# V products of two blocks first, the last MLP tile's high and low parts in one half, and twelve dummy products at the end

## The chip, the cores and the metric

One Trainium2 chip, one of its cores. The core has TensorE (PE; its weight loads are shown as PEld), VectorE (DVE), ScalarE (ACT), GpSimd (POOL) and SyncE (SP), which here only issues DMAs. The metric is the device time of one execution in microseconds (us), median of three runs.

## The reference

For x of 2048 tokens by 512, everything in float32:

```python
xn = _layernorm(x)                      # mean and variance over 512, eps 1e-5
q, k, v = split(xn @ wqkv)              # 32 heads of 16
s = softmax(q @ k.T / 4) @ v @ wo
g = silu(gelu(xn @ w1 + b1) @ w2 + b2)  # 1376 hidden columns, tanh gelu
out = x + s * g
```

## The kernel before, in words

**Precision.** A float32 operand is kept as a high part (rounded by ScalarE to the matmul's format) and a low part (operand minus high, by VectorE or GpSimd). A product is three matmuls into one PSUM bank: high x high, high x low, low x high (`mm3`, line 92).

**Start (lines 389 to 553).** x comes in 16 tiles of 128 tokens, four to a block. For each block of tiles VectorE takes the statistics (lines 414, 415), a root and a few short operations (419 to 424, the root by ScalarE at 420), and the normalised tile (428). TensorE transposes it into PSUM (437, `turn`), ScalarE writes the high part (86), VectorE the low part (87). Then come q and k for the first two groups of heads, per block of 512 tokens (455, `q_first`: 24 products), and V for tokens 0 to 511, per tile (`v_tile`, 12 products through line 92). `evac` (368 to 381) copies q/k out of PSUM on ScalarE, takes the low part on GpSimd, and SyncE stores both to scratch in DRAM. Before the first transposes, and behind them, TensorE runs products on an identity matrix (487, `keep_warm`). wv is split by ScalarE (511) and GpSimd (502). `pool_after` (499) is a tiny GpSimd operation that keeps GpSimd waiting for a given normalised tile. The order of the four blocks is: turns of block 0, q/k 0; turns 1, V tile, q/k 1; turns 2, V tile, q/k 2; turns 3; then, behind the loads described next, V tile, q/k 3, V tile.

**SyncE's order.** Every DMA of SyncE is issued in the order of the program. After the stores of q/k block 2 come `load_qs(0)` (line 146, six loads of q rows back from scratch, high and low stacked in 48 rows) and `load_k(0)` for the first 512 keys (line 121, six loads), then the first MLP weights, the next 1024 keys, the stores of q/k block 3, and the last 512 keys.

**Projection stage (lines 556 to 752).** The rest of V, the MLP and the other q/k groups run as pairs of products on the two halves of TensorE's rows, half 0 on rows 0 to 63 and half 1 on rows 64 to 127 (`run`, `mm`, line 583). Between them, one for each five of these products, `fill` puts a score product q x k (line 193, 48 rows of one half, two PSUM banks in turn), whose maximum VectorE takes (199): 590 of the 2048 in this stage, shared between the halves as evenly as possible. TensorE executes in order, so a score product that waits for its q or k rows holds up all behind it. The first score product is the fifth product of the stage. The MLP's hidden columns are 11 tiles of 128; 1376 is 10 x 128 + 96, so the last is padded with 32 zeros. `half` computes a pair of hidden tiles, `evac` applies gelu and splits, and `down` multiplies with w2: two parts for each block and hidden tile, each with two token tiles of three products on either half.

**Attention and end.** Scores again with the maximum folded in (716), exponentials (719, 721), products with V (787), then the output projection (916, 92), the gate (922), the sum with x (927) and the store (928). The last product goes through line 92 into the bank `two`; behind it are two VectorE operations of 256 columns and the store.

Where a row half must wait for the other's write to the same bank, `mm` puts a hold ahead of the product:

```python
        if not first and writer[key][0] != a and writer[key][1] > prog["seen"]:
            hold = nc.tensor.nop().ins
```

Of the kernel before, what the change touches and what calls it, by code (L numbers as in the profile page):

```python
# [16 lines left out]
P = 128  # L17
# [8 lines left out]
F = 1376  # L26
FT = (F + P - 1) // P
GH = 4
NG = H // GH
# [25 lines left out]
def fused(ctx: ExitStack, tc: tile.TileContext, x, wqk, wv, wo, w1, b1, w2, b2, out):  # L55
# [227 lines left out]
    wk = sa.enter_context(tc.tile_pool(name="work_a", bufs=2))  # L283
    b1_sb = xp.tile([P, FT], F32, name="b1_sb")
    b2_sb = xp.tile([P, D], F32, name="b2_sb")
# [47 lines left out]
    W1, W2 = {}, {}  # L333

    def w1_load(j):
        if j < len(pairs):
            for u in pairs[j]:
                kind, n, f = u
                if kind == "m":
                    W1[u] = w_new(w1[f], 2, "raw1")  # L340
                elif f % 2 == 0:
                    W1[n] = w_new(wqk[:, n], 2, "raw1")
# [8 lines left out]
    def w2_load(i):  # L351
        if i < len(ms):
            W2[ms[i][1:]] = w_new(w2[ms[i][2]], 2, "raw2")

# [9 lines left out]
    def evac(us, ph):  # L364
        raws = [wk.tile([P, CH], F32, name="hg", bufs=2) for u in us]
        for u, raw in zip(us, raws):
            if u[0] == "m":
                nc.scalar.activation(raw, ph.pop(u), AF.Gelu_apprx_tanh, bias=b1_sb[:, u[2]:u[2] + 1])  # L368
            else:
                nc.scalar.activation(raw, ph.pop(u), AF.Copy)  # L370
        for u, raw in zip(us, raws):
            hh = wk.tile([P, CH], F32R, name="hh", bufs=HB)
            hl = wk.tile([P, CH], F32R, name="hl", bufs=HB)
            nc.scalar.activation(hh, raw, AF.Copy)  # L374
            nc.gpsimd.tensor_sub(hl, raw, hh.bitcast(F32))  # L375
            if u[0] == "m":
                HS[u[1:]] = (hh, hl)
            else:
                rs, cs = slice(u[1] * P, (u[1] + 1) * P), slice(u[2] * CH, (u[2] + 1) * CH)
                nc.sync.dma_start(qk_h[rs, cs], hh.bitcast(F32))  # L380
                nc.sync.dma_start(qk_l[rs, cs], hl.bitcast(F32))
# [7 lines left out]
    with ExitStack() as s1:  # L389
# [20 lines left out]
        ve = wp.tile([P, 5, NT], F32, name="ve")  # L410

        def moments(t):
            st = w1k.tile([P, 6], F32, name="st")
            nc.vector.bn_stats(st, xs[t])  # L414
            nc.vector.bn_aggr(mv[:, t, :], st)

        def rstd(t0, t1):
            v = ve[:, :, t0:t1]
            nc.vector.tensor_scalar(v[:, 0], mv[:, t0:t1, 1], EPS, None, op0=OP.add)
            nc.scalar.activation(v[:, 1], v[:, 0], AF.Sqrt)  # L420
            nc.vector.reciprocal(v[:, 2], v[:, 1])
            nc.vector.scalar_tensor_tensor(v[:, 3], v[:, 2], -0.5, v[:, 2], op0=OP.mult, op1=OP.mult)
            nc.vector.tensor_mul(v[:, 3], v[:, 3], v[:, 0])
            nc.vector.scalar_tensor_tensor(v[:, 4], v[:, 3], 1.5, v[:, 2], op0=OP.add, op1=OP.mult)
# [22 lines left out]

        def q_first(c):
            pq = {}
            for n, (i, j) in enumerate(((0, 0), (0, 1), (1, 0))):  # L450
                for g in range(2):
                    if n == 0:
                        pq["q", g, c] = a_tile((P, CH))
                    for k in range(KT):
                        nc.tensor.matmul(pq["q", g, c], W1[g][i][:, k * P:(k + 1) * P], (xh, xl)[j][c][:, k],  # L455
                                         start=n == 0 and k == 0, stop=n == 2 and k == KT - 1)
            evac(list(pq), pq)

        for t in range(4):
            load_x(t, (nc.sync, nc.scalar)[t % 2])  # L460
        warm = wp.tile([1, 2], F32, name="warm")
        nc.vector.memset(warm, 1.0)
        nc.scalar.activation(warm[:, 1:], warm[:, :1], AF.Sqrt)
# [6 lines left out]
        for t in range(6, XB):  # L470
            load_x(t)
# [16 lines left out]

        keep_warm(25)
        def ln(t, n):  # L490
            for i in range(t, t + n):
                moments(i)
            rstd(t, t + n)
            for i in range(t, t + n):
                norm(i)

        ln(0, NCH)
        def pool_after(t):
            nc.gpsimd.tensor_sub(warm[:, :1], xns[t][:1, :1], xns[t][:1, :1])

        def wv_low(k):
            nc.gpsimd.tensor_sub(wv_l[:, k], wv_r[:, k], wv_h[:, k].bitcast(F32))

        pool_after(NCH - 1)
# [5 lines left out]
        for k in range(KT):  # L510
            nc.scalar.activation(wv_h[:, k], wv_r[:, k], AF.Copy)
        for k in range(KT - 2):
            wv_low(k)
        ln(NCH, NCH)
        consts()
        pool_after(2 * NCH - 1)
        for k in range(KT - 2, KT):
            wv_low(k)
# [31 lines left out]
    load_k(0, c0=CH, n=S - 2 * CH)  # L550
    v_tile(NCH - 2)
    q_first(NCH - 1)
    v_tile(NCH - 1)
    load_k(0, c0=S - CH, n=CH)

    prog.update(n=0, pe=0, seen=0)
    writer = {}
    s_when, row = [], [0]
    def fill(a):
        due = 2 * FILL0 + APART * sum(made)  # L560
        if sum(made) < SOON and row[0] >= due and (made[0] <= made[1]) == (a == 0):
            taken()
            if later and later[0][0] <= 0:
                s_send(later.pop(0)[1])
            whole_units = list(ended)
            s_one(a)
            for u in whole_units:
                s_end0(u)
            tick()

# [17 lines left out]
    def run(ops, hooks={}):  # L588
        for n, two in enumerate(zip(*ops)):
# [4 lines left out]
            for h in hooks.get(n, []):  # L594
                h()

    PH = {}
# [21 lines left out]
    def down(c, f, part):  # L619
# [4 lines left out]
        h, w = HS[c, f], W2[c, f]  # L624
        side = (part + i) % 2
        ops = [[], []]
        for a in range(2):
            for t in ((0, 1), (2, 3))[(a + side) % 2]:
                ts = slice(t * P, (t + 1) * P)
                for n, (x, y) in enumerate(((0, 0), (0, 1), (1, 0))):  # L630
                    ops[a].append(((c, t), PA[c][t], h[x][:, ts], w[y],
                                   f == 0 and part == 0 and n == 0, f == FT - 1 and part == 1 and n == 2))
        run(ops)
        if part == 0:
# [446 lines left out]
```

## Time and profile before

| | us |
|---|---|
| median of three runs | 1547.04 |
| the runs | 1546.8 to 1547.23 |
| span of the profiled execution, first to last instruction | 1544.6 |
| TensorE busy | 1538.4 |
| VectorE busy | 1419.2 |
| ScalarE busy | 1212.4 |
| GpSimd busy | 375.8 |

For the profiled execution the page gives the span; the median is 2.4 us more. Times in rows count from the first instruction. A row of the timeline gives start, length, engine, line, operation, output <- inputs, shapes, the count of instructions merged, and in brackets the idle time before it with what ended it. A row of the stages gives the stretch, its length, the busy time and the instruction count of PE, PEld, DVE, ACT and POOL, then the granted TensorE clock, the DMA engines' share and GB/s. TensorE works in a pipeline, so a product's length in a row (0.39 us for 512 columns) is longer than the distance to the next (0.23).

### The profile page before, as it was taken

The page shows a single profiled execution, that of the slowest core. Times are in us where ns is not written, and L with a number is a line of the kernel's source. Part 1 is how long each engine was busy: PE and PEld are TensorE (multiplying, and loading weights), DVE is VectorE, ACT ScalarE, POOL GpSimd, SP SyncE. Part 2 cuts the span into 40 slices and gives each one's busy share as a digit, 9 for nine tenths or more (in the row PEclk, how much of TensorE's full clock was granted, in tenths as well). Part 3 has the DMA queues.
Part 4 walks back from the last instruction along what each step waited for, and adds up shares of the span by engine and source line. Part 5 has one row for each costly group of instructions (what it writes and reads, how often), then busy time and mean ns, then how long its engine had stood idle before and what let it go on. Part 6 is the DMA issues. An engine that isn't in the chain of part 4 may idle for free.

```text
span 1544.6 us, 31302 instructions
## 1 busy us (share of the span) xinstructions
PE 1538.4 (100%) x12230; PEld 922.5 (60%) x12230; DVE 1419.2 (92%) x2294; ACT 1212.4 (78%) x1881; POOL 375.8 (24%) x386
## 2 busy tenths in 40 slices
PE   9999999999999999999999999999999999999998
PEld 8899999999995444444444444444444444444456
DVE  7799999999998999999999999999999999999945
ACT  4333433333339999999999999999999999999994
POOL 4235575756741011001000100100010000000153
PEclk9999999999999999999999999999999999999999
DMA  6615443455422112112411411411051111110162
GB/s 212 155 58 145 124 143 108 120 161 136 141 90 66 39 45 61 33 37 51 75 28 33 71 33 41 60 44 29 21 84 29 32 32 30 41 32 20 50 217 100
DMA packets 78227, 116.83 MB, mean 76 GB/s; under 512 B 28132, under 2 KB 28388, under 8 KB 76904
## 3 DMA queue, kind: packets, MB, share of 16 engines
q1 hardware_dynamic: 73596, 99.80, 23.1%
q0 software_dynamic: 4000, 14.45, 5.0%
q8 instruction: 96, 1.57, 0.4%
q10 hardware_dynamic: 484, 0.60, 0.1%
q14 instruction: 51, 0.42, 0.1%
HBM read 84.35 MB, written 25.97 MB: 71 GB/s over the span
## 4 chain that ended last, share of the span: by engine, by line
PE 99%; DVE 1%; DMA 0%; issue 0%; ACT 0%; DVEq 0%
PE pv L787 33%; PE ps L193 22%; PE ps L583 13%; PE two L716 8%; PE sp L583 5%; PE ps L716 4%; PE pst L716 4%; PE pst L583 3%; PE pv L583 2%; PE ps L916 2%; PE ps L92 1%; PE ps L455 1%; PE pst L92 0%; DVE st L414 0%; PE two L92 0%; DMA xt<-in_x 0%
## 5 line engine op out<-in xcount | busy, mean ns | idle before, releaser
L199 DVE TENSOR_REDUCE mx<-ps 128x2 f32<-128x512 f32 x2048 | 1318.0, 687 | 68.5 <-PE ps L193 18.3
L787 PE MATMUL pv<-slot,vsb 128*32 128x512 f32 x4096 | 543.4, 604 | 0.0
L721 ACT ACTIVATE slot<-two 128x1024 f32<-128x1024 f32 x511 | 520.5, 1019 | 0.0
L193 PEld LDWEIGHTS ps<-kt,slot 48*128 48x128 f32 x1356 | 212.2, 184 | 290.2 <-DVE mx L199 278.4
L193 PE MATMUL ps<-kt,slot 48*128 48x256 f32 (+1 forms) x1356 | 376.3, 366 | 0.0
L719 ACT ACTIVATE slot<-ps 128x512 f32<-128x512 f32 x515 | 307.5, 598 | 16.7 <-PE ps L716 7.2
L719 ACT ACTIVATE slot<-pst 128x512 f32<-128x512 f32 x511 | 309.9, 606 | 0.0
L583 PE MATMUL ps<-slot,w1h 64*128 64x512 f32 x1088 | 225.4, 392 | 0.0
L193 PE MATMUL ps<-kt,qz 48*128 48x512 f32 x512 | 202.2, 395 | 0.0
L716 PE MATMUL two<-qt,kt 50*128 50x512 f32 x766 | 197.5, 395 | 0.3 <-DVE gt L643 0.3
L716 PE MATMUL ps<-qt,kt 50*128 50x512 f32 x387 | 189.7, 492 | 0.0
L193 PEld LDWEIGHTS ps<-slot,slot 48*128 48x128 f32 x590 | 92.8, 184 | 124.0 <-DVE mx L199 118.2
L193 PE MATMUL ps<-slot,slot 48*128 48x256 f32 (+1 forms) x590 | 165.8, 366 | 0.0
L787 PEld LDWEIGHTS pv<-slot,vsb 128*32 128x32 f32 x4096 | 81.5, 108 | 131.9 <-issue 124.4
L583 PEld LDWEIGHTS ps<-slot,w1h 64*128 64x128 f32 x1088 | 154.1, 185 | 9.8
L583 PE MATMUL ps<-slot,w1l 64*128 64x512 f32 x544 | 157.0, 392 | 0.0
L716 PE MATMUL pst<-qt,kt 50*128 50x512 f32 x383 | 155.7, 406 | 0.0
L375 POOL TENSOR_TENSOR hl<-hg,hh 128x512 fp32r<-128x512 f32 x76 | 96.7, 1295 | 158.2 <-ACT hh L374 109.3
L368 ACT ACTIVATE hg<-ps,b_sb 128x512 f32<-128x512 f32 x44 | 27.9, 684 | 133.0 <-PE ps L583 121.7
L716 PEld LDWEIGHTS two<-qt,kt 50*128 50x128 f32 x766 | 114.5, 186 | 1.1 <-DVE gt L643 0.7
L246 POOL CAST mh<-nt 128x32 fp32r<-128x32 f32 x19 | 4.0, 209 | 375.7 <-DVE nt L244 322.8
L193 PEld LDWEIGHTS ps<-kt,qz 48*128 48x128 f32 x512 | 93.7, 183 | 1.0 <-DVE mx L199 0.7
(197 smaller groups left out, 1974.6 us busy)
## 6 DMA issues: line engine op xcount, KB each, us to landing
raw<-in_w SPq DMA_DIRECT2D x88, 256.0 KB
qk_h<-hh SPq DMA_DIRECT2D x32, 256.0 KB
qk_l<-hl SPq DMA_DIRECT2D x32, 256.0 KB
qt<-qk_h SPq DMA_DIRECT2D x128, 64.0 KB
slot<-qk_h SPq DMA_DIRECT2D x92, 64.0 KB
g_d<-gt POOLq DMA_DIRECT2D x16, 256.0 KB, 3.3
qt<-qk_l SPq DMA_DIRECT2D x64, 64.0 KB
dn<-den_d SPq DMA_DIRECT2D x32, 128.0 KB
```

Of the source, the lines that this page charges most:

```text
L92: nc.tensor.matmul(ps, lhs[a], rhs[b], start=first and n == 0, stop=last and n == 2)
L193: return nc.tensor.matmul(ps[:, c0:c0 + w], QS[u][r, p, qi * P:(qi + 1) * P], kts[u // NCH % KB][p][r, k0:k0 + w], start=True, stop=True).ins
L199: nc.vector.tensor_reduce(MX[u][:, 2 * p:2 * p + 2, qi, ki][:, heads, parts], ps.rearrange("p (n c) -> p n c", c=HC), axis=AX.X, op=OP.max)
L368: nc.scalar.activation(raw, ph.pop(u), AF.Gelu_apprx_tanh, bias=b1_sb[:, u[2]:u[2] + 1])
L375: nc.gpsimd.tensor_sub(hl, raw, hh.bitcast(F32))
L455: nc.tensor.matmul(pq["q", g, c], W1[g][i][:, k * P:(k + 1) * P], (xh, xl)[j][c][:, k], start=n == 0 and k == 0, stop=n == 2 and k == KT - 1)
L583: i = nc.tensor.matmul(ps, lhs[r], rhs[r], start=first, stop=last).ins
L716: nc.tensor.matmul(ps, kts[g % KB][p][r, k * P:(k + 1) * P], QT[u][r, p, :], start=True, stop=True)
L719: nc.scalar.activation(PT[u, k][:, 2 * p + a, :], ps, AF.Exp, scale=SCALE)
L721: nc.scalar.activation(PT[u, k][:, :2], TP["two"], AF.Exp, scale=SCALE)
L787: nc.tensor.matmul(PV[u][32 * j:32 * j + 32, :], vsb[:, k, h:h + 32], PT[u, k][:, j, :], start=(k == 0), stop=(k == NT - 1))
L916: HALF[0] = nc.tensor.matmul(PW[i][0], OTS[i, k][x][r], (wo_h, wo_l)[y][r, k], start=k == 0 and side == 0 and n == 0, stop=k == KT - 1 and ...
```

## The change

It has four parts. (1) At the start the first x tile is loaded in two pieces from two queues, wv's pieces are loaded ahead of wqk, statistics are taken for two tiles and then two, with one VectorE operation less, and the V products of the first two token tiles come before q/k block 0, term by term. The other two V tiles come ahead of q/k blocks 1 and 2, and the transposes of block 3 stand inside q/k block 2. (2) The last MLP tile has its 32 last columns twice in one row half: once as high part, once as low part, in the same operand, so that this half needs two products for each token tile instead of three. Its weights come in two arrangements for even and odd blocks. `run_short` orders these steps. (3) In six of the eight steps score products are put into the free places. (4) Twelve products whose result nobody reads stand behind the last real one: three of each of four kinds (128 columns, 64 columns, a broadcast operand, a strided operand).

```diff
+LAST = F - (FT - 1) * P
...
+    def form(c, f):
+        return FT if f == FT - 1 and c % 2 else f
...
             nc.scalar.activation(hh, raw, AF.Copy)
-            nc.gpsimd.tensor_sub(hl, raw, hh.bitcast(F32))
+            if u[0] == "m" and u[2] == FT - 1:
+                long, low = [(slice(0, 64), slice(LAST, P)), (slice(64, P), slice(P - LAST, 64))][u[1] % 2]
+                nc.gpsimd.tensor_sub(hl[long], raw[long], hh[long].bitcast(F32))
+                nc.gpsimd.tensor_sub(hh[low], raw[low], hh[low].bitcast(F32))
+            else:
+                nc.gpsimd.tensor_sub(hl, raw, hh.bitcast(F32))
...
+        def root(t0, t1):
+            nc.scalar.activation(ve[:, 1, t0:t1], mv[:, t0:t1, 1], AF.Sqrt, bias=eps)
...
-        def q_first(c):
+        def v_term(t, n):
+            i, j = ((0, 0), (1, 0), (0, 1))[n]
+            if n == 0:
+                VP[t] = a_tile((P, D))
+            c, ts = t // NCH, slice(t % NCH * P, t % NCH * P + P)
+            for k in range(KT):
+                nc.tensor.matmul(VP[t], (xh, xl)[i][c][:, k, ts], (wv_h, wv_l)[j][:, k],
+                                 start=n == 0 and k == 0, stop=n == 2 and k == KT - 1)
+            if n == 2:
+                v_out(t, VP.pop(t))
+
+        def q_first(c, mid=()):
...
+                    if n == 2 and g == 1:
+                        for t in mid:
+                            turn(t)
...
-        for t in range(4):
-            load_x(t, (nc.sync, nc.scalar)[t % 2])
+        xs[0] = w1k.tile([P, D], F32, name="xt", bufs=XB)
+        for eng, r in ((nc.sync, slice(0, P // 2)), (nc.scalar, slice(P // 2, P))):
+            eng.dma_start(xs[0][r], x[r, :])
+        load_x(1)
+        load_x(2, nc.scalar)
...
+        for k in range(KT):
+            if k == 2:
+                load_x(3)
+            nc.sync.dma_start(wv_r[:, k], wv[:, k])
         for g in range(2):
             W1[g] = w_new(wqk[:, g], 2, "raw1")
-        for t in range(4, 6):
-            load_x(t)
-        for k in range(KT):
-            nc.sync.dma_start(wv_r[:, k], wv[:, k])
...
-        keep_warm(25)
+        keep_warm(15)
...
-        ln(0, NCH)
...
+        moments(0)
+        moments(1)
+        root(0, 2)
+        stats(2)
+        rstd(0, 2)
+        norm(0)
+        norm(1)
+        aggr(2)
+        moments(3)
+        for k in range(KT - 1):
+            wv_high(k)
+        pool_after(1)
+        turn(0)
+        wv_high(KT - 1)
+        turn(1)
+        root(2, 4)
+        rstd(2, 4)
+        norm(2)
+        norm(3)
+        for k in range(2):
+            wv_low(k)
+        pool_after(3)
+        for k in range(2, KT):
+            wv_low(k)
         for g in range(2):
             W1[g] = w_split(W1[g], "w1", 4)
-        for t in range(NCH):
-            turn(t)
-        keep_warm(3)
...
+        v_term(0, 0)
+        v_term(1, 0)
+        v_term(0, 1)
+        turn(2)
+        v_term(1, 1)
+        turn(3)
+        v_term(0, 2)
+        v_term(1, 2)
         ln(NCH, NCH)
...
         q_first(0)
-        for c in range(1, NCH):
+        for c in range(1, NCH - 1):
             for t in range(NCH * c, NCH * c + NCH):
                 turn(t)
-            if c < NCH - 1:
-                ln(NCH * c + NCH, NCH)
-            else:
-                nc.scalar.activation(warm[:, 1:], warm[:, :1], AF.Gelu_apprx_tanh)
-                break
-            v_tile(c - 1)
-            q_first(c)
+            ln(NCH * c + NCH, NCH)
+            v_tile(c + 1)
+            q_first(c, range(NT - NCH, NT) if c == NCH - 2 else ())
+        nc.scalar.activation(warm[:, 1:], warm[:, :1], AF.Gelu_apprx_tanh)
...
     load_k(0, c0=CH, n=S - 2 * CH)
-    v_tile(NCH - 2)
     q_first(NCH - 1)
-    v_tile(NCH - 1)
     load_k(0, c0=S - CH, n=CH)
...
+    def run_short(ops, short, moved):
+        n = len(ops[1 - short])
+        for i in range(n):
+            prog["n"] += 1
+            left = n - i - len(ops[short])
+            for a in range(2):
+                if not moved:
+                    fill(a)
+                    if ops[a]:
+                        mm(a, *ops[a].pop(0))
+                elif a == short and left and (is_due() or len(ops[a]) == 0):
+                    put(a)
+                else:
+                    mm(a, *ops[a].pop(0))
+        if moved:
+            skew[0] += 2 - 4 * short
...
+        short = 1 - c % 2 if f == FT - 1 else None
...
+            xy = ((0, 0), (0, 1), (1, 0))[:2 if a == short else 3]
...
+            run_short(ops, short, c < NCH // 2 or part == 0)
...
+        if n == len(ends) - 1:
+            spin = ps_v.tile([P, CH], F32, name="pv")
+            w = wo_h[:, 0]
+            for m, mov in ((P, w), (P // 2, w), (P, wo_h[:, 0, :1].to_broadcast([P, D])),
+                           (P, w.rearrange("p (a b) -> p b a", a=2))):
+                for _ in range(3):
+                    nc.tensor.matmul(spin[:m], wo_l[:, 0, :m], mov, start=True, stop=True)
         w_gate(t, i)
```

`put` issues one score product with what belongs to it, `is_due` is the old condition of `fill` on the count of products, and `skew` lets the two halves' counts of score products differ by what was put on one side.

More of the change, by code (lines that the diff above doesn't have):

```diff
@@ L367, in evac @@
             if u[0] == "m":
-                nc.scalar.activation(raw, ph.pop(u), AF.Gelu_apprx_tanh, bias=b1_sb[:, u[2]:u[2] + 1])
+                f = form(*u[1:])
+                nc.scalar.activation(raw, ph.pop(u), AF.Gelu_apprx_tanh, bias=b1_sb[:, f:f + 1])
             else:
@@ L492, in ln @@
                 moments(i)
+            root(t, t + n)
             rstd(t, t + n)
@@ L558, in fused, with is_due, put @@
     s_when, row = [], [0]
-    def fill(a):
[L560 to L569, printed above, removed]
+    skew = [0]
+    def is_due():
+        return sum(made) < SOON and row[0] >= 2 * FILL0 + APART * sum(made)
+    def put(a):
+        taken()
+        if later and later[0][0] <= 0:
+            s_send(later.pop(0)[1])
+        whole_units = list(ended)
+        s_one(a)
+        for u in whole_units:
+            s_end0(u)
+        tick()
+    def fill(a):
+        if is_due() and (made[0] - made[1] <= skew[0]) == (a == 0):
+            put(a)
     def taken():
@@ L625, in down @@
         side = (part + i) % 2
+        short = 1 - c % 2 if f == FT - 1 else None
         ops = [[], []]
         for a in range(2):
+            xy = ((0, 0), (0, 1), (1, 0))[:2 if a == short else 3]
             for t in ((0, 1), (2, 3))[(a + side) % 2]:
                 ts = slice(t * P, (t + 1) * P)
-                for n, (x, y) in enumerate(((0, 0), (0, 1), (1, 0))):
+                for n, (x, y) in enumerate(xy):
                     ops[a].append(((c, t), PA[c][t], h[x][:, ts], w[y],
-                                   f == 0 and part == 0 and n == 0, f == FT - 1 and part == 1 and n == 2))
-        run(ops)
+                                   f == 0 and part == 0 and n == 0, f == FT - 1 and part == 1 and n == len(xy) - 1))
+        if short is None:
+            run(ops)
+        else:
+            run_short(ops, short, c < NCH // 2 or part == 0)
         if part == 0:
@@ L1057 @@
     wv = wqkv[:, 2 * D:].reshape(KT, P, D).transpose(1, 0, 2)
[L1058 to L1061 removed]
+    ends = np.arange(F - F % P, F)
+    twice = ends[64:]
+    fs = np.concatenate([np.arange(F), twice, twice, twice, ends[:64]])
+    w1 = np.asarray(B_w1)[:, fs].reshape(KT, P, FT + 1, P).transpose(2, 1, 0, 3).reshape(FT + 1, P, KT * P)
+    w2 = np.asarray(B_w2)[fs].reshape(FT + 1, P, D)
+    b1 = np.asarray(B_b1)[fs].reshape(FT + 1, P).T
     host = {
```

45 lines of the change are left out of this document (21 added, 24 removed).

## Prediction

> **What bounds the kernel now.** I read the page first: busy times and the chain of work that ended last.
>
> ```profile
> PE 1538.4 (100%) x12230; PEld 922.5 (60%) x12230; DVE 1419.2 (92%) x2294; ACT 1212.4 (78%) x1881; POOL 375.8 (24%) x386
> PE 99%; DVE 1%; DMA 0%; issue 0%; ACT 0%; DVEq 0%
> ```
>
> TensorE is busy all the span and the chain runs through it. So an edit is worth the TensorE time it takes out, plus or minus the waits it makes TensorE stand in. The change touches three places: the first 60 us, eight steps inside the projection stage, and the last 4 us. For the first I read the chain in order of time.
>
> ```profile
> 0.74 3.13 DMA xt<-in_x
> 8.53 1.92 DVE xn L428 x4
> 20.11 2.79 PE pst L92 x12
> 33.01 5.60 PE ps L455 x24
> 38.61 0.89 PE sp L437 x8
> 39.51 0.46 PE pst L437 x4
> 39.97 0.45 PE ps L437 x4
> 48.76 2.79 PE sp L92 x12
> 51.56 0.43 PE pst L583
> ```
>
> One V tile is 2.79 us of TensorE, one q/k block (two groups) 5.60 us, four transposed tiles 0.89 + 0.46 + 0.45 = 1.8 us. The third q/k block ends at 38.61. After it come transposes (1.8), V tile (2.79), q/k block (5.60), V tile (2.79), 13.0 us in all, and at 51.5 the stage of row-tile pairs begins (I call this moment T0). Those 13 us matter: during them SyncE stores the third block's results and loads the first q and k rows for the score products.
>
> ```profile
> 42.64 0.38 SPq L381 DMA_DIRECT2D qk_l<-hl  x1
> 43.20 0.32 SPq L146 DMA_DIRECT2D qz<-qk_h  x1
> 48.24 0.42 SPq L121 DMA_DIRECT2D kt<-qk_l  x1
> ```
> ```profile
> L193 PEldq EVENT_SEMAPHORE  x8: 51/51/2000, 48.2 to 51.5; - x8
> L193 PEld LDWEIGHTS ps<-kt,qz x2: 184/184/184, 51.8 to 52.3; 48*128 48x128 f32 x2
> L193 PE MATMUL ps<-kt,qz x2: 388/392/397, 52.1 to 52.5; 48*128 48x512 f32 x2
> ```
>
> The second fence is line 193, the score product, from 47 to 53 us: "duration min/median/max, first and last start". TensorE's sequencer, running ahead of the array, stood 2.0 us, from 48.2 to 50.2, until q and k rows of the first row half had landed; the waits for the second half ended by 51.5. The array was still on the last V tile, so this cost nothing: the margin to the first score product's weight load at 51.8 is 1.6 us, to the second's at 52.3 0.8 us.
>
> **The change part by part: the start.** Two things set when TensorE has real work: normalised x and split wv.
>
> ```profile
> 3.89 0.69 DVE L414 BATCH_NORM_STATS2 st<-xt 128x6 f32<-128x512 f32 x1 [3.04 <-DMA xt<-in_x]
> 4.72 0.66 DVE L414 BATCH_NORM_STATS2 st<-xt 128x6 f32<-128x512 f32 x1
> 7.72 0.18 DVE L421 RECIPROCAL ve<-ve 128x4 f32<-128x4 f32 x1 [0.27 <-ACT ve L420]
> 7.86 1.33 ACT L294 ACTIVATE w1h<-raw 128x512 fp32r<-128x512 f32 x2 [0.18 <-DMA raw<-in_wqk]
> 9.13 1.11 PE L437 MATMUL ps<-ident,xn 128*128 128x128 f32 x8 [0.22 <-DVE xn L428]
> 9.82 1.08 ACT L86 ACTIVATE slot<-ps 128x512 fp32r<-128x512 f32 x2 [0.63 <-PE ps L437]
> 13.24 2.55 POOL L502 TENSOR_TENSOR kt<-wv_r,kt 128x512 fp32r<-128x512 f32 x2
> ```
> ```profile
> 0.00:5.00 5.00, 3.64 (x17) 3.64 (x18) 1.14 (x4) 1.49 (x2) 1.83 (x8) 1.00 0.59 206
> 5.00:10.00 5.00, 4.78 (x43) 4.55 (x42) 4.45 (x15) 1.65 (x4) 0.00 (x0) 1.00 0.98 338
> ```
>
> The first transpose at 9.13 waits for statistics of four tiles (0.83 each) and the root. With two tiles first it leaves out 2 x 0.83, about 1.6 us: 7.5. Next the load order. A 256 KB load takes 0.78 us at 338 GB/s (last column of the stage rows). wv's third piece is now the seventh load. The fifth released ScalarE at 7.86, so two loads on is 9.4; by bytes alone (206 x 5.00 = 1.03 MB by 5.00, seven loads are 1.84 MB) it is 7.4. In ScalarE's queue that piece's copy stands ahead of the first transposed tile's copy. From 9.4: copy of wv to 10.0, first tile's copy to 10.5, fourth wv piece to 11.0, second tile's copy to 11.5 (0.5 apart, as L86), low part on VectorE to 12.2, four short operations (0.8) and two norms (about 0.5 each, L428) to 13.9. GpSimd's marker waits for that, then takes two low parts of wv (1.25 apart) to 16.7; the last terms of the two V blocks need them and end at 17.9; q/k block 0 ends at 23.5. From 7.4 the same chain ends at 22.3. Behind it TensorE has twelve transposed tiles, two V tiles and three q/k blocks, 5.4 + 5.6 + 16.8 = 27.8, with no wait that I find. T0 becomes 50.1 to 51.3; I take the middle, 50.8, a gain of 0.7. Without any wait it would be 7.5 + 7.2 + 11.2 + 22.4 = 48.3, the far bound of this gain. The warm-up that is cut, 20 passes, and the three products that go only filled idle time.
>
> **The load that is no longer covered.** The fourth x block's transposes move into the third q/k block and both V tiles ahead of it, so between that block's end and T0 only one q/k block is left, 5.6 us instead of 13.0. SyncE's order is unchanged: stores of the third block (they wait for its GpSimd low parts), then six q loads, six k loads. Behind the waiting score product on TensorE stands everything else, the V terms too. From 38.61 to the release at 50.2 are 11.6 us, to 51.5 12.9, to the second score product at 52.5 about 13.9, of which some 0.7 was not waiting. I take 13.2. With T0 at 50.8 the third block ends at 45.2, the first score product is let go at 56.8, and the second starts at 58.4 instead of 52.5: **+5.9 net** of the 0.7 gained. With T0 between 50.1 and 51.3 it is +5.2 to +6.4, at the far bound +3.4. The loads' own time I vary by 0.5 either way, since the same stores go ahead of them.
>
> **The clock.** That stall leaves the array idle from about T0 + 0.5 to T0 + 6.2, 5.7 us.
>
> ```profile
> 1540.00:1544.30 4.30, 0.68 (x6) 0.47 (x5) 1.47 (x4) 0.00 (x0) 0.00 (x0) 1.00 0.37 131
> 1544.30:1545.00 0.70, 0.00 (x0) 0.00 (x0) 0.00 (x0) 0.00 (x0) 0.00 (x0) 0.54 0.00 0
> ```
>
> The column before the last two is the granted clock. The last product ended at 1540.68 and the clock fell near 1544.35, 3.7 us later (0.54 is the mean over the 0.7 us). At the start (the stage rows above) 17 passes took 3.64 us, 0.214 each; in the next 5 us 43 ran, a gap included, about 0.11. So half pace lasts some 3.6 us after work resumes, and costs half of that: **+1.8**. Bounds: 0 if the clock does not fall, 3.6 if half pace lasts two such spells.
>
> [...]
>
> **The MLP's last tile.** In each of eight steps the short half issues 4 products instead of 6: 16 row-half products fewer, eight on each half.
>
> ```profile
> 100.00:150.00 50.00, 50.00 (x431) 46.18 (x428) 48.82 (x74) 17.95 (x32) 29.40 (x25) 1.00 0.50 135
> L199 DVE TENSOR_REDUCE mx<-ps 128x2 f32<-128x512 f32 x2048 | 1318.0, 687 | 68.5 <-PE ps L193 18.3
> ```
>
> 431 products in 50 us with two halves side by side is 0.232 per pair: 8 x 0.232 = 1.86 at most. In six steps score products fill the free slots; in two the long half runs on alone. [...] Score products come no denser over the stage; VectorE, nearly all maxima of 0.69, is busy 48.8 of 50 us, so it only just follows, and a burst of two is held by two banks. GpSimd takes one more pass of about 1.3 (as L502) at each of four tiles; it is busy 29.4 of 50 us, and three to four steps lie between a tile's activation and its use. Taken at 0; uncovered it would be up to 5.
>
> **The twelve dummy products.**
>
> ```profile
> 1540.40 0.28 PE L92 MATMUL two<-wo_h,slot 128*128 128x256 f32 x1
> 1541.18 0.42 DVE L927 TENSOR_TENSOR slot<-slot 128x256 f32<-128x256 f32 x1
> 1537.23 4.73 SPq L928 DMA_DIRECT2D out<-slot  x5
> 51.48 0.18 PEld L583 LDWEIGHTS pst<-kt,slot 64*128 64x128 f32 x1 [0.36 <-issue]
> ```
>
> Twelve at 0.233 (5.60 / 24) from 1540.5 end at 1543.5 with the last one's 0.4. The last store is issued until 1541.96 and the span ends at 1544.6, so they lie beside the store's flight: 0. No row shows a product with 64 columns, a broadcast or a strided operand; if these run at half pace (three more at 0.23) and each change of shape costs the 0.36 of the last row, the end is 1545: I let this cost up to 1.
>
> [...]
>
> **Sum.** +5.9 + 1.8 - 1.5 + 0 = +6.2. The profiled execution's span is 1544.6; it becomes 1550.8. The median of the runs shown, 1547.04, is 2.4 above that span, start and end outside it, which I leave as is: 1553.2. A measurement of this kernel tells 0.2%, about 3.1 us, from no change.
>
> **Rivals.** (1) *The clock stays up.* All else equal, +4.4: 1551.4. [...] Against: 5.7 us of idling against the 3.7 us after which it fell.
> (2) *No wait at the first score product*, the result not slower. This holds if q and k rows land by T0 + 0.8, that is 6.4 us after the third block instead of 12.9. Then -0.7 - 1.5 = -2.2: 1544.8, within 0.2%. Against: twelve loads 0.46 apart alone take 5.5 us of issue behind stores that wait 4 us for GpSimd. It would need the queue's order to differ from what the code says.
> (3) *The dummies gate the last output*: the last w_gate waits for TensorE's count behind them instead of the last real product. Twelve at 0.233 is +2.8 more: 1556.0. Against: the wait is for one product's result, and the twelve write another bank.
> (4) *The short half saves nothing*, since the long half still has six products: +1.5 more, 1554.7. The filled slots speak against it.
>
> **How the numbers follow.** Stall with clock loss 0.55 (1553.2); stall without it 0.25 (1551.4); no stall 0.07; dummies as gate 0.05; no saving in the last tile 0.08. The stall cases reach from +3.4 - 1.9 to +6.9 + 3.6 + 1 - 1.5. Leaving 2 in 10 out, 1549.2 to 1556.2. Below 1550.1 is 0.12 from the stall cases' low end (T0 early, no clock loss) and rival 2, and a gain of over 3.1 us would need rival 2 with T0 near its far bound: 0.04. Slower: 0.84.
>
> **What would show it.** In the changed profile: first transpose near 7.5; T0 near 50.8; an idle time of TensorE of about 6 us just before line 193's first products, with the matching long event wait; a granted clock below 1 in the 5 us behind it; the last real product of the projection stage as much later as the second score product, plus the clock's loss, less 1.5; the dummies' last product before the final store lands. If score products start within 1 us of T0, the main step is wrong; if the clock stays 1.00, only its term.

## The result, and the profile after

The changed kernel takes 1554.9 us, the median of 5 runs (1554.25 to 1555.89), beside 1547.04 (1546.8 to 1547.38) for the kernel before on the same chip: ratio 1.0052, 95% interval 1.004 to 1.0063, slower by 7.9 us. The profiled execution took 1555.05 with a span of 1553.2, so 8.6 us more span than before and 1.85 us outside it. The other runs, too, have about 1.8 us outside the span; the profiled execution of the kernel before, with its 1544.6, was therefore some 0.6 us faster than the median, which is why the spans differ by 8.6 and the medians by 7.9.

The page of the changed kernel, busy times and the shares of the chain that ended last:

```profile
PE 1541.0 (99%) x12200; PEld 920.2 (59%) x12200; DVE 1419.3 (91%) x2295; ACT 1213.5 (78%) x1882; POOL 381.3 (25%) x390
...
PE 96%; DMA 0%; DVE 0%; SPq 0%; ACT 0%; issue 0%; POOL 0%
```

TensorE still carries the chain, but its share of the span has gone from 100% to 99% and its part of the chain from 99% to 96%: it stands somewhere. Where shows in its timeline, first two rows of the kernel before, then the changed kernel:

```profile
51.49 0.50 PE L583 MATMUL pst<-kt,slot 64*128 64x512 f32 x1
...
52.07 0.39 PE L193 MATMUL ps<-kt,qz 48*128 48x512 f32 x1
```
```profile
9.38 1.11 PE L456 MATMUL ps<-ident,xn 128*128 128x128 f32 x8 [2.88 <-DVE xn L447]
10.88 4.61 PE L475 MATMUL sp<-kt,slot 128*128 128x512 f32 x12 [0.38 <-ACT slot L87]
...
44.63 0.63 PE L456 MATMUL pst<-ident,xn 128*128 128x128 f32 x4 [0.63 <-DVE xn L447]
...
46.38 1.18 PE L490 MATMUL sp<-slot,w1l 128*128 128x512 f32 x4
47.90 4.00 PE L490 MATMUL sp<-slot,w1h 128*128 128x512 f32 x16 [0.34 <-ACT hg L375]
...
53.70 0.49 PE L650 MATMUL pst<-kt,slot 64*128 64x512 f32 x1
...
59.21 0.76 PE L194 MATMUL ps<-kt,qz 48*128 48x512 f32 x1 [4.78 <-DMA kt<-qk_l]
...
60.23 0.62 PE L194 MATMUL ps<-kt,qz 48*128 48x512 f32 x1
```

The stage of row-tile pairs begins at T0 = 53.70 instead of 51.49, and the first score product (line 194 now) starts at 59.21 instead of 52.07, behind a stand of 4.78 us. SyncE's order in the changed kernel says what it stood for, the last low-part store of the third block, the first q load, and the last k load of the first group:

```profile
51.55 0.32 SPq L391 DMA_DIRECT2D qk_l<-hl  x1
52.05 0.32 SPq L147 DMA_DIRECT2D qz<-qk_h  x1
...
57.09 0.42 SPq L122 DMA_DIRECT2D kt<-qk_l  x1
```

The third q/k block ends at 47.56 (46.38 + 1.18), and the first score product starts 11.65 us later; before, the sequencer's long wait was over after 11.6 (38.61 to 50.2). These are not quite the same event, but the path through the stores and loads is unchanged to a few tenths: the first q load is issued 4.5 us behind the block (before 4.6) and the last k load 5.0 behind that (before 5.0). What has changed is that only 6.1 us of TensorE's time up to T0 lie in it, not 13.

Further down the trace the delay stays almost what it is at 60 us. The 41st score product is 8.75 us later than before, the 101st 8.74, the last product of the projection stage 8.53 (477.20 for 468.67), the last product of the attention 8.70, the span's end 8.6.

### The profile page after: what moved, and what is told of

Its sections match the earlier page's. It is cut to its first block, busy times and chain, and to the rows that moved or that the text cites. A ratio compares the mean times of both kernels' runs of the same rounds, so it can differ in the third digit from the quotient of the medians.

```text
span 1553.2 us, 31256 instructions
## 1 busy us (share of the span) xinstructions
PE 1541.0 (99%) x12200; PEld 920.2 (59%) x12200; DVE 1419.3 (91%) x2295; ACT 1213.5 (78%) x1882; POOL 381.3 (25%) x390
## 4 chain that ended last, share of the span: by engine, by line
PE 96%; DMA 0%; DVE 0%; SPq 0%; ACT 0%; issue 0%; POOL 0%
PE pv L876 33%; PE ps L194 22%; PE ps L650 13%; PE two L805 8%; PE sp L650 5%; PE ps L805 4%; PE pst L805 4%; PE pst L650 3%; PE pv L650 2%; PE ps L1005 2%; PE ps L93 1%; PE two L93 0%; DVE mx L200 0%; PE pst L93 0%; PE pv L1141 0%; DMA qz<-qk_h 0%
## 5 line engine op out<-in xcount | busy, mean ns | idle before, releaser
L650 PE MATMUL ps<-slot,w1h 64*128 64x512 f32 x1088 | 220.0, 393 | 0.0
L650 PE MATMUL ps<-slot,w1l 64*128 64x512 f32 x544 | 149.8, 392 | 0.0
L385 POOL TENSOR_TENSOR hl<-hg,hh 128x512 fp32r<-128x512 f32 x72 | 91.8, 1296 | 148.5 <-ACT hh L379 143.2
```

Of the source, the lines that this page charges most:

```text
L650: i = nc.tensor.matmul(ps, lhs[r], rhs[r], start=first, stop=last).ins
```

## The experiments

Three batches, each on one chip with its own runs of the kernel before (1547.06, 1546.86 and 1546.7 us). One table from the traces helps to read them all. Its columns: T0 (in e6 that of its extra products); the first score product; the time from the first to the 41st score product, 27.85 before, in which half clock shows; and the time from the 101st score product to the stage's last product, in which the last MLP tile shows (in e10 and e12 the score products are still catching up there, which makes it shorter).

```
kernel                        T0      1st    1st-41st   101st-end   time      against before
before                       51.49   52.07    27.85      346.83    1547.04
after                        53.70   59.21    29.46      346.62    1554.9     1.0052 [1.0040, 1.0063]
e1 dummies alone             51.85   52.42    27.82      347.01    1547.25    1.0001 [0.9993, 1.0010]
e2 MLP tile alone            51.82   52.39    27.87      346.41    1546.58    0.9997 [0.9988, 1.0006]
e3 start alone               52.94   58.47    29.38      347.01    1555.73    1.0058 [1.0042, 1.0073]
e4 order alone               52.09   58.23    30.57      346.84    1554.68    1.0050 [1.0036, 1.0064]
e5 late scores, 4.5 apart    53.29   60.28    26.93      346.46    1552.23    1.0034 [1.0021, 1.0047]
e6 busy wait                 52.90   58.42    27.99      347.04    1553.44    1.0043 [1.0027, 1.0059]
e7 x loads as before         51.88   57.55    29.47      346.45    1554.11    1.0047 [1.0029, 1.0065]
e8 25 warm-up products       52.40   57.84    30.37      346.43    1554.61    1.0051 [1.0035, 1.0067]
e9 loads covered again       57.63   58.19    27.84      346.48    1551.79    1.0032 [1.0020, 1.0043]
e10 late scores, 4.9 apart   52.96   59.94    27.63      344.35    1551.44    1.0032 [1.0020, 1.0044]
e11 e9 + x as before         56.63   57.22    27.80      346.81    1551.03    1.0030 [1.0018, 1.0041]
e12 e10 + x as before        53.21   60.19    27.56      344.50    1550.94    1.0029 [1.0017, 1.0040]
```

**Which part loses.** e1 is the kernel before with the twelve dummies only, e2 with the last MLP tile only (all of parts 2 and 3), e3 with the new start only. e4 is the kernel before with nothing but the order of TensorE's work changed, its loads, statistics and the V tiles 0 and 1 left where they were:

```diff
+            ln(NCH * c + NCH, NCH)
+            v_tile(c - 1)
+            if c == NCH - 2:
+                v_tile(c)
+                v_tile(c + 1)
+                for t in range(NT - NCH, NT):
+                    turn(t)
...
+                q_first(c)
                 break
-            v_tile(c - 1)
             q_first(c)
...
-    v_tile(NCH - 2)
     q_first(NCH - 1)
-    v_tile(NCH - 1)
```

> The kernel before with the twelve dummy products alone. Theory (they lie beside the last store): 0.0, within 0.3 us of the kernel before; their last one ends about 0.6 us ahead of the end. Rival (they hold up the last gate or the end): +0.6 to +2.8 us. By kind: if 64 columns, a broadcast or a strided operand were slower, the distance between products of that kind would be over 0.25 us; in the changed kernel the whole dozen took 2.85 us, so I expect 0.22 to 0.24 for all four.

> The kernel before with the change to the last MLP tile alone (weights, high and low parts in one half, filled places). Theory A, read from the two traces (scores 8.8 us late at the 40th, 9.8 at the 590th, 8.5 behind the stage): waits at changes of row half eat most of it, -0.3 us, between -0.6 and 0. Theory B (the prediction's term): -1.5 us, and the loss inside the stage came only from the late start.

> The kernel before with the changed start alone (loads, statistics two by two, V products first, transposes inside the third q/k block). Theory: all of the loss is here, +8.2 to +9.0 us: first row-tile stage 2.2 later, a stand of about 5 us at the first score product, a spell of half clock. Rival (the last MLP tile or the dummies hold part of it): under +7 us.

> The kernel before, where only the order on TensorE is changed: the last block's transposes and the last two V tiles stand ahead of the third q/k block, and nothing but the fourth q/k block is left between it and the row-tile stage. Loads, statistics and warm-up as before. Theory (the score product waits for loads that the moved work had covered): the row-tile stage starts within 1 us of before, then the first score product stands 4.5 to 6 us, the clock falls for one spell, together +5.5 to +7.5 us. Rival (the loss comes from the late start itself, not from the order): within 1 us of the kernel before.

e1 gives 1547.25, no difference; e2 1546.58, within its interval no difference either; e3 1555.73, the whole loss. And e4, the order alone, loses 7.6 us, with T0 only 0.6 later than before; that is just over what was expected of it, and the half clock came for two spells instead of one. The stand is the same thing in both, here the first score product of e3 and then that of e4:

```profile
58.47 0.76 PE L193 MATMUL ps<-kt,qz 48*128 48x512 f32 x1 [4.80 <-DMA kt<-qk_l]
```
```profile
52.09 0.49 PE L585 MATMUL pst<-kt,slot 64*128 64x512 f32 x1
...
58.23 0.76 PE L193 MATMUL ps<-kt,qz 48*128 48x512 f32 x1 [5.42 <-DMA kt<-qk_h]
```

So neither the load order of x and wv nor the split statistics are needed for the loss: it is enough to put V tiles and transposes ahead of a q/k block whose results have to come back through DRAM.

**The clock as a term of its own.** e6 is the changed kernel with twenty products on 64 rows ahead of the stage, which need no q or k rows and whose result nobody reads:

```diff
+    busy, ring = s_tile()[0], s_ring
+    for _ in range(20):
+        nc.tensor.matmul(busy, xh[0][:64, 0, :P], xh[0][:64, 0], start=True, stop=True)
     k_ones(kts[0])
```

> The changed kernel with twenty products on 64 rows, read by nobody, ahead of the first product of the row-tile stage (20 x 0.23 = 4.7 us, inside the stand of 4.9 us). The score product comes at the same time as before; what changes is that TensorE does not idle. Theory (the half clock behind the stand is a term of its own): clock 1.00 there and -1.1 to -2 us against the changed kernel, 1553 to 1553.8. Rival (the clock costs nothing that counts, or falls all the same): 1554.5 to 1555.5.

It ran in 1553.44, 1.5 less than the changed kernel, though the two intervals overlap. What the clock costs is read from the traces. The stages show it (third column from the right), first of the changed kernel at the start and around the stand, then of e6:

```profile
8.00:11.40 3.40, 1.64 (x10) 1.32 (x11) 3.04 (x11) 2.63 (x6) 1.46 (x3) 1.00 1.06 399
11.40:14.80 3.40, 3.40 (x9) 2.65 (x9) 2.39 (x8) 1.65 (x4) 1.63 (x3) 0.50 0.48 178
59.00:62.40 3.40, 3.19 (x16) 2.76 (x18) 1.38 (x2) 0.00 (x0) 0.00 (x0) 0.53 1.04 343
```
```profile
56.00:59.00 3.00, 2.77 (x17) 2.01 (x16) 0.08 (x1) 0.00 (x0) 0.85 (x1) 1.00 0.76 188
59.00:62.40 3.40, 3.40 (x31) 3.32 (x30) 3.21 (x5) 0.00 (x0) 0.00 (x0) 1.00 1.07 315
```

Behind the stand the changed kernel starts 16 products in 3.4 us, e6 31. From the first to the 41st score product it needs 29.46, e6 27.99, the kernel before 27.85: one spell of half clock costs 1.5 us. The loads end no earlier for being waited for by a busy array: e6's first score product still starts only at 58.42, 5.5 us behind its T0 of 52.90, as in the changed kernel (59.21 and 53.70). Its T0 is 0.8 earlier for another reason, told next, and part of the 1.5 us by which e6 ran faster can come from there.

**Why the stage starts late.** e7 loads the first four x tiles as the kernel before does, wv still ahead of wqk; e8 has 25 warm-up products instead of 15.

```diff
-        xs[0] = w1k.tile([P, D], F32, name="xt", bufs=XB)
-        for eng, r in ((nc.sync, slice(0, P // 2)), (nc.scalar, slice(P // 2, P))):
-            eng.dma_start(xs[0][r], x[r, :])
-        load_x(1)
-        load_x(2, nc.scalar)
+        for t in range(4):
+            load_x(t, (nc.sync, nc.scalar)[t % 2])
...
-            if k == 2:
-                load_x(3)
```

> The changed kernel with the first four x tiles loaded as in the kernel before (whole tiles, on both queues in turn, ahead of wv); wv still ahead of wqk. Theory (the third x tile, landing at 7.4, held VectorE's row of operations and with it the first norm): first transpose at 7.3 to 7.9 instead of 9.4; the row-tile stage starts 0.5 to 2 us earlier, and so does the end. Rival (wv's pieces and GpSimd's low parts set the start): first transpose earlier, stage no more than 0.3 us earlier.

> The changed kernel with 25 warm-up products instead of 15, so that TensorE is busy until about 8.7 us. Theory (the idle 2.9 us ahead of the first transpose let the clock fall at 11.4 in the profiled run): clock 1.00 in the first 50 us, the row-tile stage starts up to 1 us earlier, -0.3 to -1 us. Rival (the fall has nothing to do with the warm-up): no change.

VectorE in the changed kernel, the third tile's statistics and the first norms:

```profile
7.40 0.69 DVE L426 BATCH_NORM_STATS2 st<-xt 128x6 f32<-128x512 f32 x1 [1.62 <-DMA xt<-in_x]
...
8.78 1.00 DVE L447 TENSOR_SCALAR xn<-xt,mv,ve 128x512 f32<-128x512 f32 x2
```

The program puts `stats(2)` ahead of `rstd(0, 2)` on VectorE, to fill the wait for ScalarE's root. The third tile landed only at 7.4, so the norms of tiles 0 and 1, which needed nothing of it, stood 1.62 us behind it. In the kernel before four tiles' statistics were done by 7.2. e7 takes this away:

```profile
7.94 1.11 PE L456 MATMUL ps<-ident,xn 128*128 128x128 f32 x8 [0.51 <-DVE xn L447]
...
51.88 0.50 PE L645 MATMUL pst<-kt,slot 64*128 64x512 f32 x1
...
57.55 0.60 PE L194 MATMUL ps<-kt,qz 48*128 48x512 f32 x1 [4.94 <-DMA kt<-qk_h]
```

The first transpose comes at 7.94, T0 at 51.88 and the first score product at 57.55: 1.4, 1.8 and 1.7 earlier than in the changed kernel. The stand stays. In the time there is 0.8 of this, inside the interval. Not all of the 1.8 is the third tile's, since e7 has no early half clock either (11.4 to 14.8 in the changed kernel). e8 has none, T0 1.3 earlier, but then two spells behind its stand, so its time is the same. The stages of e8:

```profile
56.00:60.00 4.00, 2.16 (x10) 1.99 (x12) 0.73 (x2) 0.00 (x0) 0.30 (x1) 0.55 0.77 249
60.00:64.00 4.00, 4.00 (x24) 3.37 (x24) 2.44 (x4) 0.00 (x0) 0.00 (x0) 0.60 1.07 226
```

But e3, e6 and e10 have no early half clock with 15 warm-up products; e3, for one:

```profile
10.00:15.00 5.00, 4.31 (x20) 3.29 (x21) 3.07 (x10) 3.46 (x8) 2.85 (x4) 1.00 0.67 245
```

So e8 does not show that the extra warm-up products kept the clock up, and its third x tile happened to land 0.8 earlier (6.53 instead of 7.33 in e6), which can account for its T0 of 52.40. What the early spell costs shows between runs of one and the same start: with it T0 is 53.70 (changed kernel; in e5, with a spell from 9.0 to 12.4, 53.29), without it 52.94, 52.90 and 52.96 (e3, e6, e10). In e6 the first transpose comes at 9.32, as late as in the changed kernel, and T0 0.8 earlier. Measured against these three, the x order of e7 gives 1.0 us of T0, not 1.8.

**Is it enough to ask for the rows later?** e5 and e10 let the first score product be due 60 products into the stage, and then one for each 4.5 or 4.9 products until the old pace of one for each five is met. The pace after that, and the count of 590, are the same.

```diff
-        return sum(made) < SOON and row[0] >= 2 * FILL0 + APART * sum(made)
+        return sum(made) < SOON and row[0] >= max(2 * FILL0 + APART * sum(made), 60 + 4.5 * sum(made))
```

> The changed kernel, where the first score product is due after 60 products of the row-tile stage instead of 4 (about 7 us later), and the following ones after each 4.5 products until they have caught up with one for each 5. Same work. Theory (TensorE stands only because the score product waits for q and k rows): no stand, no half clock at that place, -5.5 to -7 us against the changed kernel, so 1548 to 1549.5. Rival (the late start of the stage is the loss): within 1 us of the changed kernel, 1554 to 1556.

> The changed kernel with the first score product due 60 products into the stage, as in the run with late score products, but with one for each 4.9 products after that instead of 4.5. Theory (in that run VectorE was the limit: 0.687 for a maximum, while a score product came each 0.64): at 4.9 a score product comes each 0.685, just what VectorE can do, so TensorE keeps its 43 to 44 products in 5 us and only a little is given back: 1549.4 to 1551.5, with 130 or more products in each 15 us from 65 to 125 us. Rival (maxima put off cannot be made up at all, or the shifted score products cost for another reason): 1552 or more, as with 4.5.

Both have no stand and no half clock there, and e5 should have been 5.5 to 7 faster than the changed kernel. It was 2.7 faster. Three windows of 30 us, of the kernel before, of e5 and of e10:

```profile
65.00:95.00 30.00, 30.00 (x260) 26.63 (x258) 29.50 (x44) 7.63 (x14) 6.08 (x5) 1.00 0.15 43
```
```profile
65.00:95.00 30.00, 30.00 (x246) 26.43 (x246) 29.49 (x45) 5.45 (x11) 5.07 (x4) 1.00 0.34 96
```
```profile
65.00:95.00 30.00, 30.00 (x258) 27.35 (x257) 29.29 (x44) 7.64 (x14) 5.54 (x5) 1.00 0.33 95
```

TensorE counts as busy all the time, but in e5 it started 246 products and not 260: 14 x 0.116 = 1.6 us lost in each 30. VectorE is the likely reason: it was busy 29.5 of 30 us in the kernel before already, and with a score product due each 4.5 + 1 products, 5.5 x 0.116 = 0.64 us, it is asked for a maximum each 0.64. The products that stretch in e5 are the score products, which write the banks that VectorE has to free: 444 ns on the mean from 53 to 130 us, while the others stay at 390 to 393. What VectorE managed in e5 from the 41st to the 101st was 40.70 / 60 = 0.678. The kernel before takes 41.92 / 60 = 0.699 there. So a maximum that is put off is made up at 0.02 us apiece. e5's spacing meets the old one after (60 - 4) / 0.5 = 112 score products, which gives back 2.4 us of the 6.4 by which the first one comes later behind T0; the other 4 remain, and the stage ends 5.7 later than before with T0 1.8 later. e10 asks for one each 5.9 x 0.116 = 0.684, which by e5's 0.678 VectorE could follow. It took 41.72 / 60 = 0.695, and 1551.44, at the upper end of what was expected: it lost less in each stretch, but over more of them. Whether it is VectorE or the irregular change between the row halves that takes the last 0.01 us, these runs don't tell.

**Covering the load again.** e9 puts the transposes of block 3 behind q/k block 2 and the V tiles 2 and 3 around q/k block 3, as in the kernel before; V tiles 0 and 1 (token tiles of 128, the "two blocks" of the title) stay ahead of q/k block 0. e11 is e9 with x loaded as before, 25 warm-ups and no dummies, meant to beat both kernels; e12 is e10 with the same additions.

```diff
             ln(NCH * c + NCH, NCH)
-            v_tile(c + 1)
-            q_first(c, range(NT - NCH, NT) if c == NCH - 2 else ())
+            q_first(c)
+        for t in range(NT - NCH, NT):
+            turn(t)
...
+    v_tile(2)
     q_first(NCH - 1)
+    v_tile(3)
     load_k(0, c0=S - CH, n=CH)
```

> The changed kernel with one part put back: the transposes of block 3, a V tile, q/k block 3 and a V tile stand again between the third q/k block and the row-tile stage, with the loads in front as in the kernel before; the V products of tiles 0 and 1 stay ahead of q/k block 0. Theory (the uncovered load makes the stand): the 4.8 us stand at the first score product, the half clock behind it (1.05) and the two short waits of 0.63 and 0.34 go, about 6.7 us: 1548.2, from 1547.3 to 1549.3, with the stage's start at 52.7 and the clock at 1.00 behind it. Rival (the new start is the loss by itself, the stand only shows it): 1553 or more, with another wait of over 3 us ahead of the first score product.

> The changed kernel with the loads covered as in the first kernel of this set, the first four x tiles loaded as in the kernel before, 25 warm-up products, and no dummy products; the V products of tiles 0 and 1 first and the last MLP tile as changed. Theory: no stand, stage start 1.8 earlier than with the changed x order, near 51.4, and the MLP's 0.5: 1546.4, from 1545.4 to 1547.4, so no slower than the kernel before. Rival (V products first cost in themselves): over 1548.5.

> The changed kernel with the gentle late score products, the first four x tiles loaded as in the kernel before, 25 warm-up products, and no dummies. Theory: the second kernel of this set less 1.4 to 1.8 from the earlier stage start: 1547.8 to 1550. Rival (the earlier stage start is spent in a wait for q and k rows, since the first score product comes 7 us into the stage and the rows 6 us): a stand of more than 1 us at the first score product, or no gain over the second kernel.

TensorE's timeline of e9:

```profile
27.37 5.54 PE L490 MATMUL ps<-slot,w1h 128*128 128x512 f32 x16 [1.92 <-ACT slot L87]
...
38.50 3.99 PE L490 MATMUL ps<-slot,w1h 128*128 128x512 f32 x16 [1.98 <-ACT slot L87]
...
57.63 0.49 PE L653 MATMUL pst<-kt,slot 64*128 64x512 f32 x1
...
58.19 0.39 PE L194 MATMUL ps<-kt,qz 48*128 48x512 f32 x1
```

The stand is gone: the first score product follows T0 by 0.56 us, at full clock. So the stand was the uncovered load, and the forecast of 1548.2 wrong all the same: e9 takes 1551.79. Two new waits of 1.92 and 1.98 us have come, ahead of q/k blocks 1 and 2, for the split of the transposed tiles into high and low part, and behind the first the clock fell (0.50 from 27.54 to 30.95): 16 products took 5.54 us there and otherwise take 3.89. Together that is 5.5 us. In both kernels a V tile, 2.8 us, stood in each of these places and hid the split. There are four V tiles. The kernel before spends them on blocks 1, 2 and 3 and on the loads at the end. Two put to the front leave two for these places, and either the splits show (e9) or the loads do (the changed kernel, 4.8 and the clock).

e11 and e12 gain 0.8 and 0.5 on e9 and e10, inside their intervals, miss their forecasts of 1546.4 and 1547.8 to 1550, and are slower than the kernel before by 0.3%. They do not test the old x order: VectorE normalises x from 7.28 us on in e11, as from 7.34 in e7, but the 25 warm-up products hold TensorE until its first transpose at 9.66, which follows them without a wait (9.68 in e12, and 7.94 in e7 with 15). T0 of e12 is 53.21, no earlier than e10's. No version with the new start beats it; e2, without that start, equals it.

## Why the prediction was right, step by step

Predicted: 1553.2 from +6.2. Measured: 1554.9 by medians, +8.6 in span. The likeliest case, stall with clock loss, is the one that came: that part of the mechanism was right, and e4 and e9 show it. That the sum came within 1.7 us is partly luck. Two terms made it too low, T0 (a gain of 0.7 where 2.2 were lost) and the MLP tile (1.3 less was saved). Three made it too high, the way from the third block to the second score product (by 0.5), the clock (by 0.8) and the time outside the span (2.4 taken, about 1.8 in the runs).

```
term                                        predicted   measured   from
second score product against before          +5.9        +7.7      60.23 - 52.52
  of it: end of the third q/k block          45.2        47.56
  of it: block end to first score product    11.6        11.65
  of it: block end to second                 13.2        12.67
half clock behind the second                 +1.8        +1.0      41st score 8.75 late
last MLP tile                                -1.5        -0.2      8.53 at the stage's end
attention                                     -          +0.2      8.70 at its end
dummies                                       0           0.0      8.6 in span, page to 0.1
```

**The stall** was sized by one measured distance, third block to release, and that came out within a few tenths. e4 shows it alone and e9 shows it gone. The long event wait named as a sign did not come: the eight waits at line 194 last 0.05 us each, from 58.3 on, and the stand shows only as idle time.

**The start** is the term that was mis-sized most: "T0 becomes 50.1 to 51.3; I take the middle, 50.8, a gain of 0.7". T0 came at 53.70, 2.2 later than before. The step that failed is the first transpose at "7.5": it left out two tiles' statistics, as the program does, but took the third tile's for free, although they stand ahead of the root's followers in VectorE's queue and wait for a load. The chain had a second hole, a clock that fell at 11.4 behind a wait of 2.88 us for the normalised x (the twelve V products took 4.61 us; at full clock in e6 3.12). The end of q/k block 0 tells the two apart. The prediction had 22.3 to 23.5 for it. It came at 24.72 in the changed kernel, at 23.93 to 23.98 in e3, e6 and e10, which have the same start without the spell, and at 22.91 in e7, which has neither the spell nor the wait for the third tile: 0.8 for the clock, 1.0 for the tile. From there to T0 it is 29.0 instead of 27.8. Together that is the 2.9 by which T0 was missed, to 0.1. Of the last 1.2, 0.97 are what "with no wait that I find" overlooked, the waits of 0.63 and 0.34 us in q/k blocks 2 and 3.

**The clock** fell for one spell, as the likeliest case had it, and costs 1.5 us from the first score product on by e6; 1.0 of it comes behind the second, where the sum put 1.8. Two spells, the upper bound, came in e4 and e8, with 30.57 and 30.37 to the 41st score product, 2.5 to 2.7 above 27.85.

**The last MLP tile** was taken at -1.5 and gives far less. Of the 1.86 us that the pace of the products allows at most, the forecast took off 0.36 for waits at seven more changes of half; no run shows such a wait, and in place of the 1.5 the runs show 0.3. Without the change the way from the 101st score product to the stage's end is 346.83, 347.01, 347.01 and 346.84 us (before, e1, e3, e4), with it 346.41 to 347.04 (e2, after, e6, e7, e8, e9, e11), on the mean 0.3 less. 16 products fewer are there in the trace (2960 for 2976 on the row halves). Where their 1.86 us go is partly seen: from 122 to 464 us e2 starts 2921 products and the kernel before 2927, and six product times are 0.7 us. What holds those was not tried apart: the seven more changes of half, the shifted score products, or VectorE, which has the same 590 maxima to take and is busy 332.7 of these 342 us in e2 and 332.8 before.

**The dummies** cost nothing. In the tail of the changed kernel they begin before VectorE's last two operations and end before the last store lands:

```profile
1549.11 0.28 PE L93 MATMUL two<-wo_h,slot 128*128 128x256 f32 x1
1549.23 2.85 PE L1141 MATMUL pv<-wo_h,wo_l 128*128 128x512 f32 x12
...
1549.43 0.42 DVE L1011 SCALAR_TENSOR_TENSOR slot<-two,slot 128x256 f32<-128x256 f32 x1
1549.89 0.42 DVE L1016 TENSOR_TENSOR slot<-slot 128x256 f32<-128x256 f32 x1
```

The gate operation starts 0.2 us after the first dummy, so the rival by which it waits for all twelve is out, and e1 agrees.

Of the rivals, the one with no wait at the first score product fails by 4.8 us and the one in which the clock stays up by 1.5. That the short half saves nothing is nearly so; the free slots are filled in six of the eight steps, yet the time isn't gained, and whether the long half sets the pace, as that rival had it, was not tried.

## What to carry to other kernels

Work that is needed some time is also cover for something: before moving it, list what it hides in its old place, and measure that path from the trace (here 11.6 us from a block's end to its rows' return). An operation put into a waiting engine's queue as a filler is only free if its own input is there (here the norms stood 1.62 us behind the third tile). And where a second engine is as busy as VectorE here (29.5 of 30 us), a delay of the work that feeds it is made up only slowly by asking for it faster (0.02 us for each maximum here).

## What the runs showed of the hardware that was not expected

The half-clock spells lasted 3.41 us (changed kernel, 11.42 to 14.84 and 59.21 to 62.62) or 6.83 (e4 and e8), whatever the stand's length between 4.7 and 5.4 us. The 6.83, two spells on end, came in the two runs in which the stand reached far into the first: TensorE was busy 2.40 of its 3.41 us in e4 and 1.96 in e8, and 3.15 or more where one spell was all (changed kernel, e3, e5, e7, e9). The changed kernel's first spell began 2.0 us after the products had resumed at 9.38, at the end of a stretch, 8.0 to 11.4 in the stages above, in which TensorE was busy 1.64 of 3.40 us: there the clock fell with the array in partial use. In e5 it fell behind 1.40 of 3.41 us (5.57 to 8.98) and in e9 behind 1.50 of 3.42 (24.12 to 27.54). In e3, e6 and e10, with the same start, it stayed up: 1.00 from 0 to 20 us in e3, and 1.000 on the mean of the whole profiled execution in e6 and e10. So one and the same start lost its clock in some executions and kept it in others, and what decides it these runs do not show.

The dummies of four kinds, with 128 columns, 64 columns, a broadcast and a strided operand, followed one another at 0.233, 0.23, 0.22 and 0.217 us in the trace. From the last of a kind to the first of the next it was 0.23, 0.22 and 0.22 us, so no gap stands at the change to 64 columns or at the two others.
